# Moving one addition of VectorE's exponential into an accumulating DMA, and giving VectorE more score banks

## The chip, the cores and the metric

The kernel runs on one core of one Trainium2 chip. The metric is the device time of one execution in microseconds (us). "Before" and "after" are the kernel before and after the change. A ratio is the mean time of one kernel's fast runs over the mean time of the other's in the same rounds, so it is not quite the ratio of the medians that stand beside it. The profile of a kernel is of one execution, and its span is some 2 us shorter than the time.

## The reference, cut to what matters

```python
def _A_ref(x, wqkv, wo):                     # x: 1 x 2048 x 512, 32 heads of 16
    qkv = (x @ wqkv).reshape(B, S, 3, H, Dh).transpose(2, 0, 3, 1, 4)
    q, k, v = qkv[0], qkv[1], qkv[2]
    scores = einsum("bhqd,bhkd->bhqk", q, k) * (Dh ** -0.5)
    o = einsum("bhqk,bhkd->bhqd", softmax(scores), v)
    return o.transpose(0, 2, 1, 3).reshape(B, S, D) @ wo
def _B_ref(x, w_gate, w_up, w_down):         # F = 1792
    return (silu(x @ w_gate) * (x @ w_up)) @ w_down
g = sigmoid((x * gate_w).sum(-1, keepdims=True))
return g * _A_ref(...) + (1 - g) * _B_ref(...)
```

What costs is the softmax: 32 x 2048 x 2048 exponentials. With 16 numbers in a head, the matmuls are small beside them.

## The kernel before

Scores are made in banks of 128 keys x 512 queries of one head, 2048 banks in all. 32 units of 64 banks each (four heads, 512 queries, 16 tiles of keys) follow one another. Two engines share the exponentials. ScalarE takes two banks in one instruction:

```python
def emit_pair(bs):                            # two banks, ScalarE
    s_t = ps_s.tile([P, 2 * QBW], F32, tag="s", name="s_t")    # PSUM, 2 buffers
    e_t = etp.tile([P, 2 * QBW], BF16, tag="e", name="e_t")
    for k, b in enumerate(bs):
        score(s_t[:, k * QBW:(k + 1) * QBW], b)                # the two use different halves of the array
        ...
    act(out=e_t[:], in_=s_t[:], func=ACT.Exp, scale=inv_sqrt_dh)
```

VectorE takes single banks and works on four of them, a block, at a time. Its exponential builds the bits of a bf16 number as an integer: a first pass from PSUM (y), then six passes over 2048 elements that correct the mantissa (z, u).

```python
def emit_d(b):                                # one bank, VectorE
    d_t = ps_d.tile([P, QBW], F32, tag="d", name="d_t")        # PSUM, 1 buffer
    score(d_t[:, :], b)
    ...
    def first():
        vec.tensor_scalar(out=y[:, i * QBW:(i + 1) * QBW], in0=d_t[:, :], scalar1=EXP_A, scalar2=EXP_B, ...)
        if i < NV - 1:
            return                            # NV = 4
        z = vex.tile([P, NV * QBW], U16, tag="z", name="z_t")  # pool vex: 1 buffer; y has 3
        u = vex.tile([P, NV * QBW], F16, tag="u", name="u_t")
        vops.extend([
            (0.73, lambda: vec.tensor_scalar(out=za, in0=ya, ...)),         # z: mantissa bits
            (0.73, lambda: vec.tensor_scalar(out=ua, in0=za, ...)),         # u = K z + M
            (1.26, lambda: vec.tensor_tensor(out=ua, in0=ua, in1=ua, op=ALU.mult)),
            (1.26, lambda: vec.tensor_tensor(out=ua, in0=ua, in1=za, op=ALU.mult)),
            (1.26, lambda: vec.tensor_tensor(out=ya, in0=ya, in1=ua, op=ALU.add)),
            (0.73, lambda: (vec.tensor_scalar(out=ya, in0=ya, ...),         # the closing pass
                            late.append((plan.dve + 0.4, mine)))),
        ])
```

The output product (o_ps) of a unit takes the exponentials as they come; a block that is ready only after its unit has closed goes into a bank of its own (x_ps), which VectorE adds later.

All engines run fixed lists of instructions. A planner in the kernel's Python makes them: it keeps three clocks (plan.pe, plan.dve, plan.act), gives every instruction a planned cost, and fills TensorE's spare time with "pieces" of the other work: projections of q, k and v, the bound that is subtracted in the softmax (from keys: kb, kneg; product: bp), the feed-forward part (gp, up, dps) and the output projection (a_ps). How many banks VectorE gets is not written anywhere; it follows from the clocks and this function:

```python
def to_vector():
    un, at_ = divmod(nxt, 4 * KT)
    ...
    if nxt < 16 or at_ > (50 if un < UNITS - 1 else 12) or y_live[0] >= 3 or sum(v[0] for v in vops) > 6:
        return 0
    return 1
```

## Time and profile before

866.77 us (median of 3 runs, 866.67 to 867.56).

| engine | busy | share | what it does most |
|---|---|---|---|
| ScalarE (ACT) | 842.4 us | 97% | 880 exponentials of two banks |
| VectorE (DVE) | 797.0 us | 92% | 72 blocks of four banks |
| TensorE (PE) | 787.3 us | 91% | scores, output product, projections, feed-forward |
| GpSimd (POOL) | 8.7 us | 1% | setup |

One more reading is used throughout: the distances between the starts of ScalarE's instructions. The usual distance when nothing waits is 0.904 us after an exponential and 0.478 after a tanh (the least is 1 or 2 ns shorter). What a distance has over that is waiting, visible as idle time or hidden inside the instruction. Summed from 18 us to the last instruction of ScalarE this "stall" is 18.5 us before.

### The profile page before, as it was taken

How to read it: one execution, taken by the hardware profiler on the slowest of the kernel's cores; microseconds unless marked ns; L12 is line 12 of the kernel's file. 1: busy time of each engine (PE TensorE's matmuls, PEld its weight loads, DVE VectorE, ACT ScalarE, POOL GpSimd, SP SyncE). 2: the span in 40 equal slices, each digit the busy share in tenths (PEclk: the TensorE clock that was granted, in tenths of full speed). 3: DMA queues.
4: the chain of work that ended last, by engine and by line, in shares of the span. 5: the costliest groups of instructions: out<-in, count | busy, mean ns of one | idle time of the engine just before them, and what ended most of it. 6: DMA issues, size and time to landing. Idle time of an engine off the chain costs nothing.

```text
span 864.8 us, 14339 instructions
## 1 busy us (share of the span) xinstructions
PE 787.3 (91%) x5145; PEld 217.4 (25%) x5232; DVE 797.0 (92%) x1119; ACT 842.4 (97%) x945; POOL 8.7 (1%) x31
## 2 busy tenths in 40 slices
PE   5999999999999999999999898999989988889986
PEld 2222222222222222222222222222222222222222
DVE  7899999999999999999999999999999999999995
ACT  4999999999999999999999999999999999999996
POOL 3000000000000000000000000000000000000000
PEclk9999999999999999999999999999999999999999
DMA  8400012211210012211001121110001121100000
GB/s 201 122 1 12 9 34 48 43 44 38 47 32 8 17 38 73 54 44 41 4 7 27 39 62 38 50 47 8 1 14 42 33 65 43 27 10 4 6 20 25
DMA packets 88064, 31.99 MB, mean 37 GB/s; under 512 B 75648, under 2 KB 87544, under 8 KB 87992
## 3 DMA queue, kind: packets, MB, share of 16 engines
q1 hardware_dynamic: 86264, 30.74, 14.4%
q8 instruction: 41, 0.67, 0.3%
q10 hardware_dynamic: 1728, 0.33, 0.2%
q14 instruction: 31, 0.25, 0.1%
HBM read 20.83 MB, written 2.34 MB: 27 GB/s over the span
## 4 chain that ended last, share of the span: by engine, by line
PE 41%; ACT 39%; DVE 9%; issue 9%; SPq 1%; DMA 1%; DVEq 0%; ACTq 0%
ACT e_t L161 36%; PE s_t L158 15%; PE o_ps L158 7%; PE d_t L158 4%; DVE y_t L167 4%; PE dps L158 4%; ACT th L161 3%; PE gp L158 3%; DVE u_t L167 2%; PE up L158 2%; PE kp L158 1%; PE vp L158 1%; DVE mt L167 1%; PE qp L158 1%; PE x_ps L158 1%
## 5 line engine op out<-in xcount | busy, mean ns | idle before, releaser
L161 ACT ACTIVATE e_t<-s_t 128x1024 bf16<-128x1024 f32 x880 | 822.5, 1137 | 1.9 <-PE s_t L158 0.8
L158 PE MATMUL s_t<-qx,kaug 64*128 64x512 bf16 x1648 | 331.1, 382 | 44.3 <-ACT e_t L161 39.5
L167 DVE TENSOR_SCALAR y_t<-d_t 128x512 uint16<-128x512 f32 x288 | 198.0, 688 | 30.8 <-PE d_t L158 27.1
L158 PEld LDWEIGHTS <-kaug 64*128 64x128 bf16 x2048 | 109.7, 93 | 380.9 <-issue 376.8
L158 PE MATMUL o_ps<-e_t,vaug 128*32 128x512 bf16 x1760 | 169.9, 386 | 0.5 <-ACT e_t L161 0.5
L158 PE MATMUL d_t<-qx,kaug 64*128 64x512 bf16 x272 | 102.8, 378 | 0.9 <-DVE y_t L167 0.3
L167 DVE TENSOR_TENSOR y_t<-y_t,u_t 128x2048 uint16<-128x2048 uint16 x72 | 87.7, 1218 | 1.0
L167 DVE TENSOR_TENSOR u_t<-u_t 128x2048 f16<-128x2048 f16 x72 | 87.8, 1219 | 0.9
L167 DVE TENSOR_TENSOR u_t<-u_t,z_t 128x2048 f16<-128x2048 f16 x72 | 87.6, 1217 | 0.3
L158 PEld LDWEIGHTS <-vaug 128*32 128x32 bf16 x2048 | 43.9, 94 | 118.9 <-issue 115.7
L158 PE MATMUL dps<-wd_t,mt 128*128 128x512 bf16 x205 | 63.5, 384 | 2.5 <-issue 2.5
L158 PE MATMUL gp<-xT,wg 128*128 128x512 bf16 x202 | 62.9, 384 | 2.4 <-issue 2.4
L158 PE MATMUL up<-xT,wu 128*128 128x512 bf16 x205 | 60.9, 383 | 2.1 <-issue 2.1
L167 DVE TENSOR_SCALAR y_t<-y_t 128x2048 uint16<-128x2048 uint16 x72 | 49.6, 689 | 1.1
L167 DVE TENSOR_SCALAR u_t<-z_t 128x2048 f16<-128x2048 uint16 x72 | 49.4, 686 | 0.7
L167 DVE TENSOR_SCALAR z_t<-y_t 128x2048 uint16<-128x2048 uint16 x72 | 49.4, 686 | 0.2
L167 DVE SCALAR_TENSOR_TENSOR gs<-th,gp 128x512 bf16<-128x512 bf16 x56 | 38.3, 683 | 4.3 <-ACT th L161 3.9
L167 DVE SCALAR_TENSOR_TENSOR mt<-gs,up 128x512 bf16<-128x512 bf16 x56 | 38.2, 683 | 3.4 <-PE up L158 2.2
L161 ACT ACTIVATE th<-gp 128x512 bf16<-128x512 f32 x56 | 40.3, 720 | 0.0
L158 PEld LDWEIGHTS <-mt 128*128 128x128 bf16 x263 | 16.2, 98 | 41.1 <-issue 34.2
L158 PE MATMUL s_t<-on,kaug 64*128 64x512 bf16 x112 | 22.1, 383 | 2.6 <-ACT e_t L161 2.0
L167 DVE TENSOR_TENSOR osb<-of,x_ps 128x512 bf16<-128x512 f32 x30 | 20.4, 680 | 1.2 <-PE x_ps L158 1.2
(103 smaller groups left out, 346.9 us busy)
## 6 DMA issues: line engine op xcount, KB each, us to landing
wg<-in_B_w_gate_dram SPq DMA_DIRECT2D x56, 128.0 KB
wu<-in_B_w_up_dram SPq DMA_DIRECT2D x56, 128.0 KB
on<-osb SPq DMA_DIRECT2D x120, 16.0 KB
rb<-rr SPq DMA_DIRECT2D x15, 128.0 KB
wd_t<-in_B_w_down_dram SPq DMA_DIRECT2D x1, 1792.0 KB
qx<-qst SPq DMA_DIRECT2D x112, 16.0 KB
out_dram<-o_t SPq DMA_DIRECT2D x12, 128.0 KB
kaug<-on SPq DMA_DIRECT2D x20, 64.0 KB
```

What stands on the lines that cost most here:

```text
L158: ordered(nc.tensor.matmul(*args, **kw))
L161: ordered(nc.scalar.activation(*args, **kw))
L167: return lambda *a, **kw: ordered(f(*a, **kw))
```

## The change

VectorE's addition of y and u (72 passes) goes to the DMA engines: GpSimd's queue sends a DMA from u to y that adds. VectorE is to use the freed passes for more banks. As the DMA still reads u while the next block wants to write it, u alternates with the keys of group 0 once those are dead, from bank 320 of 2048 on.

```diff
+    u_turn = [0]
+    ADD_US = 6.0
...
-            u = vex.tile([P, NV * QBW], F16, tag="u", name="u_t")
+            u_turn[0] ^= 1
+            if u_turn[0] and nxt >= 4 * KT * QB + 4 * KT:
+                ua = kaug[:, 0, :].bitcast(F16)
+            else:
+                ua = vex.tile([P, NV * QBW], F16, tag="u", name="u_t")[:, :]
...
-                (1.26, lambda: vec.tensor_tensor(out=ua, in0=ua, in1=za, op=ALU.mult)),
-                (1.26, lambda: vec.tensor_tensor(out=ya, in0=ya, in1=ua, op=ALU.add)),
-                (0.73, lambda: (vec.tensor_scalar(out=ya, in0=ya, ...), late.append(...))),
             ])
+            def add():
+                vec.tensor_tensor(out=ua, in0=ua, in1=za, op=ALU.mult)
+                nc.gpsimd.dma_start(out=ya, in_=ua, accum_op=ALU.add)
+                added.append((plan.dve + ADD_US, last))
+            def last():
+                vec.tensor_scalar(out=ya, in0=ya, scalar1=EXP_D, scalar2=0.25, op0=ALU.add, op1=ALU.mult)
+                late.append((plan.dve + 0.4, mine))
+            vops.append((1.26, add))
...        # the planner may run other VectorE work until the DMA is due; the last stage's acc moves from kaug to mt
```

More of the change, by code (lines that the diff above doesn't have):

```diff
@@ L604 @@
     vops = []
+    added = []
+    u_turn = [0]
+    ADD_US = 6.0
     pv_turn = [True]
@@ L668, in first @@
             z = vex.tile([P, NV * QBW], U16, tag="z", name="z_t")
-            u = vex.tile([P, NV * QBW], F16, tag="u", name="u_t")
-            ya, za, ua = y[:, :], z[:, :], u[:, :]
+            u_turn[0] ^= 1
[3 more added lines that the diff above has]
+                ua = vex.tile([P, NV * QBW], F16, tag="u", name="u_t")[:, :]
+            ya, za = y[:, :], z[:, :]
             mine = list(block["b"])
@@ L678, in first @@
                 (1.26, lambda: vec.tensor_tensor(out=ua, in0=ua, in1=ua, op=ALU.mult)),
-                (1.26, lambda: vec.tensor_tensor(out=ua, in0=ua, in1=za, op=ALU.mult)),
-                (1.26, lambda: vec.tensor_tensor(out=ya, in0=ya, in1=ua, op=ALU.add)),
-                (0.73, lambda: (vec.tensor_scalar(out=ya, in0=ya, scalar1=EXP_D, scalar2=0.25, op0=ALU.add,
-                                                  op1=ALU.mult),
-                                late.append((plan.dve + 0.4, mine)))),
-            ])
+            ])
+            def add():
[6 more added lines that the diff above has]
+            vops.append((1.26, add))
         d_wait.append((plan.pe + 0.25, first))
@@ L696, in pay_v, with pay_a @@
         f()
+    def pay_a():
+        ready, f = added.pop(0)
+        plan.dve = max(plan.dve, ready) + 0.63
+        f()
     def fill_dve():
@@ L702, in fill_dve @@
                 pay_d()
+            elif added and added[0][0] <= plan.dve:
+                pay_a()
             elif owed and owed[0][0] <= plan.dve + 0.1:
@@ L706, in fill_dve @@
                 pay_v()
-            elif d_wait or owed:
-                t = min([w[0] for w in d_wait] + [o[0] for o in owed[:1]])
+            elif d_wait or owed or added:
+                t = min([w[0] for w in d_wait] + [o[0] for o in owed[:1]] + [a[0] for a in added[:1]])
                 if t > plan.pe:
@@ L837, in f @@
                     if g1 < G and not acc:
-                        acc.append(kaug[:, 0:2, :].rearrange("p g s -> p (g s)").bitcast(F32)
+                        acc.append(mt[:, 4:12, :].rearrange("p f q -> p (f q)").bitcast(F32)
                                    .rearrange("p (t d) -> p t d", d=D))
@@ L1089, in next_pv @@
         while pv_ready(None) is None:
-            pay_v() if vops else pay_d() if d_wait else pay()
+            pay_v() if vops else pay_d() if d_wait else pay() if owed else pay_a()
         emit_pv()
@@ L1144 @@
         nxt += 2
-    while closed < UNITS or late or vops:
+    while closed < UNITS or late or vops or added:
         fill_dve()
```

## The prediction

> **What bounds the kernel now.** I read the page first: busy time by engine, then the groups.
>
> ```profile
> span 864.8 us, 14339 instructions
> PE 787.3 (91%) x5145; PEld 217.4 (25%) x5232; DVE 797.0 (92%) x1119; ACT 842.4 (97%) x945; POOL 8.7 (1%) x31
> ...
> L161 ACT ACTIVATE e_t<-s_t 128x1024 bf16<-128x1024 f32 x880 | 822.5, 1137 | 1.9 <-PE s_t L158 0.8
> ...
> L167 DVE TENSOR_SCALAR y_t<-d_t 128x512 uint16<-128x512 f32 x288 | 198.0, 688 | 30.8 <-PE d_t L158 27.1
> ...
> L167 DVE TENSOR_TENSOR y_t<-y_t,u_t 128x2048 uint16<-128x2048 uint16 x72 | 87.7, 1218 | 1.0
> ...
> L167 DVE TENSOR_SCALAR y_t<-y_t 128x2048 uint16<-128x2048 uint16 x72 | 49.6, 689 | 1.1
> ```
>
> The reader is to see three engines within 55 us of one another. ScalarE does 880 exponentials of two score banks each; VectorE does the other 288 banks, in 72 blocks of four (880 x 2 + 288 = 2048). ScalarE leads: outside a start of some 18 us and an end of some 8 us it is hardly ever idle. But a busy ScalarE may still be waiting inside an instruction, so I took the timeline of ScalarE alone, from 300 us on.
>
> ```profile
> 301.90 0.72 ACT L161 ACTIVATE th<-gp 128x512 bf16<-128x512 f32 x1
> ...
> 308.38 9.40 ACT L161 ACTIVATE e_t<-s_t 128x1024 bf16<-128x1024 f32 x10
> 317.48 0.78 ACT L161 ACTIVATE th<-gp 128x512 bf16<-128x512 f32 x1
> ...
> 365.01 4.84 ACT L161 ACTIVATE e_t<-s_t 128x1024 bf16<-128x1024 f32 x5
> 370.06 6.69 ACT L161 ACTIVATE e_t<-s_t 128x1024 bf16<-128x1024 f32 x7 [0.22 <-PE s_t L158]
> ```
>
> Ten exponentials from 308.38 to 317.48 are 0.91 us each; five from 365.01 to 370.06 are 1.01. Over the whole trace the smallest and commonest distance between two starts is 0.904 us, the mean of those followed by another exponential 0.923. So each costs 0.904 when its scores are there, and over some 820 such distances 15 us are waiting that the busy figure hides. That is all a better-fed ScalarE could win beside fewer exponentials.
>
> Last the waits, of the whole trace and then of 20 to 150 us alone.
>
> ```profile
> PE s_t L158 <- ACT e_t L161: 41.5, 108, 0.7
> DVE y_t L167 <- PE d_t L158: 27.1, 64, 1.1
> ...
> PE s_t L158 <- ACT e_t L161: 4.8, 13, 0.5
> ```
>
> TensorE waits 41.5 us for ScalarE to free a score tile; that is its slack. In 20 to 150 us, with the projections, only 4.8 of it remain: there all three engines are full, and a delay on VectorE has nowhere to go.
>
> **What the Trainium skill says.** "VectorE: DVE Perf Modes", section "The perf-mode tier table (the rule you actually need)", gives 1224 ns for a 2048-element 16-bit operation of two tensors and 693 ns for one with scalars; the trace has 1218 and 689, and agrees. "DMA: Bandwidth & Descriptors", section "Anatomy of one DMA — SWDGE (gpsimd) path", fits 2.0 us plus bytes over 436 GB/s to a DMA of GpSimd's queue. "Collectives: The Full Stack", section "The bandwidth ceiling: the fold count and why AG ≠ RS ≠ AR", says that a DMA add is not slow as an addition, but needs two source reads and so about halves the rate. "SBUF — State Buffer", section "Who interferes with whom", says that GpSimd and VectorE share a port pair: while VectorE runs a scalar pass in a two-port mode, GpSimd cannot write descriptors, and the other way round; whoever starts first blocks the other. The kernel before has no DMA on GpSimd's queue, so its trace can show none of these last three.
>
> **The change part by part.** I built the changed kernel and counted its instructions on each engine.
>
> Removed: 72 additions x 1.218 = 87.7 us of VectorE. Spent again: the number of blocks is 82, ten more. On VectorE that is 40 more first passes x 0.688 = 27.5; ten times three scalar passes and two multiplications, 10 x (3 x 0.688 + 2 x 1.218) = 45.0; and 17 more additions of the late output bank (of<-of,x_ps, 23 in place of 6) x 0.68 = 11.6, because a block that is ready later misses its unit more often. Sum: 84.1. VectorE is left as full as before, at some 793 us.
>
> ScalarE: 40 banks are 20 exponentials fewer, 860 in place of 880. 20 x 0.904 = 18.1 us. As ScalarE sets the pace nearly everywhere, all of it would come off the time: 866.8 - 18.1 = 848.7. This is the ceiling of the gain, 2.1%.
>
> TensorE: a pair of banks for ScalarE goes through two halves of the array at once; the same two for VectorE go one by one. Successive groups in the timeline show about 0.22 us each, so 20 pairs fewer and 40 single ones more are +4.4, and ten more groups of the output product +2.2: together +6.6, while the span shrinks by 18. Of the 41.5 us of slack some 17 remain (41.5 - 18.1 - 6.6). TensorE then runs late for ScalarE more often; I allow 2 us.
>
> Added: 82 accumulating DMAs of 128 x 2048 x 2 bytes, 524 kB. An estimate from the two DMA sections: 2.0 + 2 x 524/436 = 4.4 us. The trace gives a longer one: the 4096-byte packets of the copies into kaug, SBUF to SBUF, took 0.33 us in the median. An even split of 128 rows over 16 engines is eight each, 2.7 us, twice that with the second read 5.3, and with the fixed 2.0 it is 7.3. The change itself plans 6.0. I take 5.5, open from 4.4 to 7.5.
>
> Where does VectorE wait for it? It runs in a fixed order, so I added the durations of the rows above over the instructions standing between. (a) Between the second multiplication, after which the DMA goes out, and the closing pass on its result there are 6.9 us in the median, under 5.8 in a tenth of the 82. With 5.5 us the shortage sums to 4 us; with 7 to 31; with 8 to 94. (b) Up to some 140 us there is one buffer u, so the next block's first write of u waits for the DMA still reading it. Nine such writes have a wait on the DMA, and 3.4, 4.1, 2.8, 3.4, 2.1, 2.8, 2.9, 4.3 and 4.8 us of work ahead of them. At 5.5 us the shortage is 2.1 + 1.4 + 2.7 + 2.1 + 3.4 + 2.7 + 2.6 + 1.2 + 0.7 = 18.9 us. VectorE's own idle time there (3 us in 50) takes some 7; two score tiles in flight hide about half of the rest. I allow 5.5 us of the time, in the stage where nothing has slack. Afterwards u alternates with the keys of group 0, and the shortest distance is 7.9 us: no loss.
>
> Sum: 866.8 - 18.1 + 5.5 (one u) + 2 (TensorE) + 1.5 (closing passes, port) = 857.7, say 858.
>
> **The rivals.** First, the whole gain arrives: 848 or a little less, if the DMA lands in 4.5 us. For it speaks that VectorE's chain is only 9% of the chain that ended last; against it the nine writes of (b). Second, the DMA is slow and VectorE becomes the bound: at 8 us, 94 us of shortage against some 54 us of idle time gives 890 or more, and each further us adds up to 82. For it speaks the packet time of kaug; against it that those packets came from several copies at once into few partitions. Third, the port: if each DMA and one scalar pass hold each other up by 0.3 us, VectorE gets 25 us more, and the time is about 868. For it speaks that 246 passes are of the two-port kind; against it that the passes reading PSUM and those of two tensors are not. Fourth, TensorE becomes the bound: 794 of 848 us is 94%, and this would leave about 855.
>
> **Range and chances.** The low end, 846, is the full gain and a little of the hidden 15 us; the high end, 885, a DMA near 7.5 us. Faster by over 2% means under 849.4, which needs all of the 18.1 us: 0.2. Slower by over 2%, above 884, needs a DMA of 7.5 us or more, or a strong fight over the port: 0.22. Within 2%: 0.58.
>
> **What would show it.** 860 exponentials in the ScalarE group, still about 0.904 us apart in full stretches; no y_t<-y_t,u_t; VectorE's busy time near 793. Waits of VectorE for a DMA before u_t<-z_t in the first 140 us, of 10 to 20 us in all, and few before y_t<-y_t. TensorE's wait for e_t down to about 17. Long waits before y_t<-y_t over the whole span would say that the DMA takes over 7 us; passes of 2048 elements longer than 0.689 would say that the port is fought over. It is wrong if ScalarE shows idle time in the middle, or if its 860 exponentials are spaced wider than 0.93.

## More of the kernel before

A piece has a deadline. One that is still missing when a unit needs it is forced, in one go and in front of everything else.

## The result

896.16 us (median of 4 runs, 893.52 to 897.96) against 866.74 before: ratio 1.0332, 95% interval 1.0313 to 1.0352. Slower, and above the range that was predicted (846 to 885).

From the page of the kernel after: busy time, TensorE's granted clock in 40 slices (in tenths), the groups of instructions (busy, mean ns | idle before, what ended it), and the DMA issues (KB, median us from issue to landing):

```profile
span 896.2 us, 14636 instructions
...
PE 819.2 (91%) x5232; PEld 220.6 (25%) x5232; DVE 789.6 (88%) x1154; ACT 829.8 (93%) x925; POOL 84.7 (9%) x113
...
PEclk9999899999999999899999999999999989999999
...
L161 ACT ACTIVATE e_t<-s_t 128x1024 bf16<-128x1024 f32 x860 | 807.9, 1106 | 38.4 <-PE s_t L158 36.8
...
L167 DVE TENSOR_SCALAR y_t<-d_t 128x512 uint16<-128x512 f32 x328 | 225.0, 686 | 45.0 <-PE d_t L158 41.4
...
L167 DVE TENSOR_SCALAR y_t<-y_t 128x2048 uint16<-128x2048 uint16 x82 | 56.1, 685 | 0.7 <-DMA y_t<-u_t 0.6
L167 DVE TENSOR_SCALAR u_t<-z_t 128x2048 f16<-128x2048 uint16 x47 | 32.4, 689 | 17.5 <-DMA y_t<-u_t 16.9
...
y_t<-u_t POOLq DMA_DIRECT2D x47, 512.0 KB, 4.8
y_t<-kaug POOLq DMA_DIRECT2D x35, 512.0 KB, 4.8
```

The counts are as built: 860 exponentials on ScalarE, 328 banks on VectorE, VectorE's busy time 789.6 us. But ScalarE, which hardly ever waited before, is idle 38.4 us in front of exponentials, and TensorE is what it waits for. TensorE in turn waited 41.5 us for ScalarE before; the waits of the kernel after (total, times, longest) show where that slack went:

```profile
ACT e_t L161 <- PE s_t L158: 36.8, 43, 5.0
PE s_t L158 <- ACT e_t L161: 19.1, 55, 0.9
DVE u_t L167 <- DMA y_t<-u_t: 16.9, 8, 3.9
ACT scaled L161 <- PE a_l L158: 8.0, 1, 8.0
```

Four stretches of both kernels, before first (stretch, its length, busy us and instructions of PE, PEld, DVE, ACT, POOL, granted clock, DMA share, GB/s):

```profile
50.00:200.00 150.00, 141.29 (x965) 41.23 (x979) 140.48 (x201) 149.93 (x170) 0.00 (x0) 1.00 0.13 29
400.00:600.00 200.00, 185.91 (x1191) 49.66 (x1211) 188.05 (x255) 199.90 (x226) 0.00 (x0) 1.00 0.13 32
```

```profile
50.00:200.00 150.00, 130.42 (x865) 35.42 (x864) 124.12 (x183) 133.34 (x145) 12.12 (x13) 0.94 0.31 61
400.00:600.00 200.00, 189.41 (x1226) 50.73 (x1224) 185.76 (x264) 198.45 (x225) 19.65 (x21) 1.00 0.44 89
```

In 400 to 600 us the change does what it was made for: ScalarE is as full as before, and the DMA is not felt. In 50 to 200 us ScalarE does 25 instructions fewer than before in the same time, and TensorE's clock is at 0.94. So the loss is not spread out; it comes in a few places. ScalarE's stall, by the measure above, in the two kernels:

| stretch, us | before | after |
|---|---|---|
| 18 to 50 | 0.7 | 1.1 |
| 50 to 200 | 1.8 | 21.5 |
| 200 to 400 | 4.4 | 14.7 |
| 400 to 600 | 3.1 | 5.0 |
| 600 to the last exponential | 5.3 | 14.9 |
| after the last exponential | 3.3 | 8.3 |
| sum | 18.5 | 65.6 |

Three kinds of place carry it. The first lies before 165 us. This is the timeline of the kernel after at its worst one (start, length, engine, instruction, idle time before and what ended it):

```profile
90.27 0.69 DVE L167 TENSOR_SCALAR u_t<-z_t 128x2048 f16<-128x2048 uint16 x1 [3.86 <-DMA y_t<-u_t]
...
91.62 0.58 PE L158 MATMUL d_t<-on,kaug 64*128 64x512 bf16 x1 [4.01 <-DVE y_t L167]
...
93.11 0.61 PE L158 MATMUL s_t<-on,kaug 64*128 64x512 bf16 x2
...
93.81 1.02 ACT L161 ACTIVATE e_t<-s_t 128x1024 bf16<-128x1024 f32 x1 [4.97 <-PE s_t L158]
```

VectorE waits 3.86 us for the DMA that still reads the one u. The pass behind it in VectorE's list would have freed d_t, so TensorE stands 4.01 us at the next score for VectorE, in front of scores that ScalarE needs; ScalarE stands 4.97 us. And a pair of scores then takes 0.61 us, not 0.39: TensorE runs at half its clock.

The second kind is at 209 us, and similar at 706 to 722:

```profile
203.69 1.04 PE L158 MATMUL qp<-xT,wqk 128*128 128x512 bf16 x4
...
206.24 2.28 DVE L167 TENSOR_REDUCE kb<-on 128x1 f32<-128x2048 bf16 x1
208.55 0.23 DVE L167 TENSOR_SCALAR kneg<-bsel,kb 128x8 bf16<-128x8 bf16 x1
...
208.84 0.38 PE L158 MATMUL bp<-aq,kneg 128*8 128x512 bf16 x1 [4.11 <-DVE kneg L167]
```

The query projection, the bound on the keys and the bound product come directly one behind the other. They had been put off until the unit needed them, and were forced: TensorE waits 4.11 us for VectorE's reduction, with nothing put between.

The third is the end. After the last exponential (ends at 880.75 us) the kernel after still has a row of feed-forward and output products to do, and ScalarE's next instruction comes late:

```profile
879.84 1.47 PE L158 MATMUL dps<-wd_t,mt 128*128 128x512 bf16 x6
...
881.57 1.04 PE L158 MATMUL dps<-wd_t,mt 128*128 128x512 bf16 x4
...
882.44 0.81 PE L158 MATMUL a_ps<-wo_t,on 128*128 128x512 bf16 x3
...
883.45 1.47 PE L158 MATMUL a_ps<-wo_t,on 128*128 128x512 bf16 x6 [0.20 <-DVE bblk L167]
...
888.79 0.69 ACT L161 ACTIVATE scaled<-a_l,gval 128x512 f32<-128x512 f32 x1 [8.04 <-PE a_l L158]
```

Before, nothing of the kind is left, and the same instruction follows the last exponential after 3.08 us:

```profile
859.52 0.69 ACT L161 ACTIVATE scaled<-a_l,gval 128x512 f32<-128x512 f32 x1 [3.08 <-PE a_l L158]
```

Counting while the programs are built agrees: the change leaves 20 matmuls of pieces for the end and forces 13 pieces; before it is none and 2.

Theories for the experiments. **A**: the single u of the first part is the loss. **B**: the 40 extra banks are; they cost TensorE time that it did not have, so pieces are put off until they are forced or left over. **C**: the DMA disturbs by itself, through the shared queues or GpSimd's port. **D**: each wait of TensorE costs again through its clock. The clock that the trace records in the kernel after is 0.5 in eight stretches of 3.4 or 6.8 us, at 73, 90, 134, 158, 209, 360, 718 and 892 us, that is right after the waits shown; before it is 0.5 once, in the last 5 us.

### The profile page after: what moved, and what is told of

It reads as the page before. It is cut to its first block, busy times and chain, and to the rows that moved or that the text cites. A ratio compares the mean times of both kernels' runs of the same rounds, so it can differ in the third digit from the quotient of the medians.

```text
span 896.2 us, 14636 instructions
## 1 busy us (share of the span) xinstructions
PE 819.2 (91%) x5232; PEld 220.6 (25%) x5232; DVE 789.6 (88%) x1154; ACT 829.8 (93%) x925; POOL 84.7 (9%) x113
## 5 line engine op out<-in xcount | busy, mean ns | idle before, releaser
L161 ACT ACTIVATE e_t<-s_t 128x1024 bf16<-128x1024 f32 x860 | 807.9, 1106 | 38.4 <-PE s_t L158 36.8
L167 DVE TENSOR_SCALAR y_t<-d_t 128x512 uint16<-128x512 f32 x328 | 225.0, 686 | 45.0 <-PE d_t L158 41.4
L158 PE MATMUL d_t<-qx,kaug 64*128 64x512 bf16 x312 | 119.8, 384 | 8.3 <-DVE y_t L167 5.6
L690 POOL DMA_DIRECT2D y_t<-u_t x47 | 43.3, 921 | 443.6 <-PE s_t L158 182.2
L690 POOL DMA_DIRECT2D y_t<-kaug x35 | 32.7, 935 | 341.1 <-PE s_t L158 236.6
L167 DVE TENSOR_TENSOR u_t<-u_t 128x2048 f16<-128x2048 f16 x47 | 57.3, 1220 | 0.7
L167 DVE TENSOR_TENSOR u_t<-u_t,z_t 128x2048 f16<-128x2048 f16 x47 | 57.2, 1217 | 0.3
L167 DVE TENSOR_SCALAR u_t<-z_t 128x2048 f16<-128x2048 uint16 x47 | 32.4, 689 | 17.5 <-DMA y_t<-u_t 16.9
L167 DVE TENSOR_TENSOR kaug<-kaug 128x2048 f16<-128x2048 f16 x35 | 42.6, 1218 | 0.3
L167 DVE TENSOR_TENSOR kaug<-kaug,z_t 128x2048 f16<-128x2048 f16 x35 | 42.6, 1216 | 0.1
```

Source lines behind the costliest of these rows:

```text
L158: ordered(nc.tensor.matmul(*args, **kw))
L161: ordered(nc.scalar.activation(*args, **kw))
L167: return lambda *a, **kw: ordered(f(*a, **kw))
L690: nc.gpsimd.dma_start(out=ya, in_=ua, accum_op=ALU.add)
```

## The experiments

The eleven runs are summed up first, beside the two kernels; "stall" is the measure above, from each profile. u: buffers for u in the first part. The runs were made in three groups on three chips (e1 to e4, e5 to e8, e9 to e11), where the kernel before took 866.6, 867.4 and 866.6 us; from one group to another the ratios compare better than the medians. A profile is one execution: that of the change is the slowest of its four (897.96 us), that of e1 the fastest (878.14).

| kernel | blocks | exponentials | u | DMA | median us | ratio to before | stall us |
|---|---|---|---|---|---|---|---|
| before | 72 | 880 | 1 | no | 866.7 | 1 | 18.5 |
| after | 82 | 860 | 1 | yes | 896.16 | 1.0332 | 65.6 |
| e1_two_u | 82 | 860 | 2 | yes | 878.99 | 1.0142 | 46.1 |
| e2_fewer | 73 | 878 | 1 | yes | 891.70 | 1.0285 | 44.0 |
| e3_two_u_fewer | 73 | 878 | 2 | yes | 873.11 | 1.0073 | 24.7 |
| e4_idle_dma | 72 | 880 | 1 | idle | 868.99 | 1.0023 | 18.5 |
| e5_filler | 82 | 860 | 2 | yes | 876.88 | 1.0108 | 44.8 |
| e6_79 | 79 | 866 | 2 | yes | 860.90 | 0.9922 | 22.7 |
| e7_79_early | 79 | 866 | 2 | yes | 863.41 | 0.9946 | 23.7 |
| e8_80 | 80 | 864 | 2 | yes | 862.99 | 0.9952 | 28.4 |
| e9_no_add | 82 | 860 | 1 | left out | 870.80 | 1.0050 | 39.5 |
| e10_79_no_add | 79 | 866 | 2 | left out | 856.21 | 0.9877 | 20.7 |
| e11_79_due | 79 | 866 | 2 | yes | 857.25 | 0.9894 | 19.4 |

### e1_two_u: a second u from the start

```diff
+            elif u_turn[0]:
+                ua = mt[:, 10:14, :].rearrange("p f q -> p (f q)").bitcast(F16)
```

> The changed kernel with a second buffer u from the first block on (four slices of the mlp tile, free until then); every engine keeps its instruction order. Theory A (the one u of the first 165 us is the main loss: VectorE waits there, TensorE idles behind it and its clock falls to half for 3.4 to 6.8 us each time): VectorE's waits of 16.9 us before u_t<-z_t go to under 2, no half-clock stretch before 165 us, ScalarE's extra spacing in 50 to 200 us falls from 21.5 us to under 5, time 872 to 880. Theory B (TensorE is overfull with the 40 extra banks, its other work is put off until it is forced): the waits before u go but the time falls by less than 8 us, to 888 or more.

Measured: 878.99 us (878.14 to 879.80), 17.2 under the change. All engines keep their order, so this is the one wait's worth. From the groups of VectorE:

```profile
L167 DVE TENSOR_SCALAR u_t<-z_t 128x2048 f16<-128x2048 uint16 x41 | 28.2, 687 | 0.6
```

The wait of 16.9 us is gone. ScalarE's stall from 50 to 200 us fell from 21.5 to 11.3 us rather than under 5, partly because the forced bound of 209 us now comes earlier, at 192, inside that stretch; and there is one half-clock stretch before 165 us, at 99 us. A holds: of the 47 us of added stall 19.5 go, and 17.2 us of the time. B is not refuted: 879 is still 30 us above what 860 exponentials would allow.

### e2_fewer and e3_two_u_fewer: no more blocks than before

```diff
-        if nxt < 16 or at_ > (50 if un < UNITS - 1 else 12) or ...
+        if nxt < 16 or at_ > (38 if un < UNITS - 1 else 12) or ...
```

> The changed kernel with 73 blocks in place of 82 (third blocks of a unit are begun later), one u as in the change. 878 exponentials. Theory B: no matmuls of the feed-forward part are left for the end, the tail after the last exponential is 8 to 9 us as before (15 in the change), the stall of 4 us at 209 us and those at 706 to 724 go; the losses of the first 165 us stay: time 878 to 886 in spite of 18 more exponentials. Theory A alone: nothing is gained, the 18 exponentials cost 16 us, 905 or more.

> Both: two buffers u and 73 blocks. If A and B together are the whole of the loss, ScalarE is again the bound with 878 exponentials, 860 to 867. If the accumulating DMA costs by itself (slower small loads, the port), 870 to 880.

Measured: 891.70 and 873.11 us. Both miss what was expected. In e2 the end is as before (3.5 us before ScalarE's last instruction) and the stalls around 706 to 724 are gone, as B said. The stall at 209 us did not go: TensorE still waits 2.7 us there for the bound on the keys (4.1 in the change). And VectorE, with 9 blocks fewer to do, waits more for the DMA:

```profile
DVE u_t L167 <- DMA y_t<-u_t: 22.2, 7, 5.5
```

The wait for u is 22.2 us in place of 16.9. A second u saves 18.6 us here (891.70 to 873.11) and 17.2 with 82 blocks: A's part is the same in both, so A and B add up. From 82 to 73 blocks the time falls by 4.5 (one u) or 5.9 us (two), while 18 more exponentials cost 16.3 (18 x 0.904). So the nine last blocks bring stall of 21 to 22 us for the 16 that they save: they are a loss by themselves. The 873 of e3 is above the 867 that A and B alone would allow; its largest stall, 4.1 us at 187 to 193 us, is again the forced bound on the keys, which this limit on blocks did not move.

### e4_idle_dma: the DMA beside the kernel before

```diff
+    nc.gpsimd.memset(mt[:, 10:14, :], 0.0)
...
                 late.append((plan.dve + 0.4, mine)),
+                nc.gpsimd.dma_start(out=idle, in_=ya.bitcast(F16), accum_op=ALU.add)
...
+            idle = kaug[:, 0, :].bitcast(U16) if nxt >= 4 * KT * QB + 4 * KT else mt[:, 10:14, :]...
```

> The kernel before, with its addition on VectorE, plus 72 accumulating DMAs of the same size into bytes that nobody reads, sent after each block's last pass. Theory C (the DMA slows the kernel by the queues' or the port's sharing alone): 872 or more, with TensorE or VectorE waiting for small DMAs, or passes of 2048 elements longer than 0.69 us. Otherwise: within 3 us of 866.7.

Measured: 868.99 us (867.79 to 869.78), ratio 1.0023 (1.0007 to 1.0038). The stall is 18.5 us, that of the kernel before. VectorE's passes of 2048 elements took 688 to 693 ns with scalars (686 to 689 before) and 1215 to 1218 with two tensors (1217 to 1219 before). C in its plain form falls: 72 such DMAs, 22.9% of the DMA engines' time for GpSimd's queue, cost the kernel before some 2 us (2.0 by the ratio).

The profile shows where 1.4 of them are: from ScalarE's last output DMA to the end of the span it is 4.2 us here and 2.8 before. All engines meet at the end, and GpSimd goes on 1.3 us after the others are done. The end is longer in every kernel that sends these DMAs, 4.2 to 5.1 us, and in none of the three without them (2.8). The fight over the port is there, but small. Where one of VectorE's scalar passes of 2048 elements fell into the first 0.85 us of GpSimd's DMA instruction (44 of 72), this took 1167 ns in the median, elsewhere 859. Of VectorE's passes that met such an instruction, 12 took 720 to 842 ns; no other took more than 696. The means hide it: 693, 689 and 688 ns for the three scalar passes, 686, 686 and 689 before.

### e5_filler: TensorE kept busy through its wait

```diff
         st["p"] = m_tile("bp")
+        for _ in range(16 if (qb, b) == (0, 2) else 0):
+            mm(st["p"][:, :], lhsT=xT[:, 0, 0:P], rhs=xT[:, 0, 0:QBW], start=True, stop=True)
         mm(st["p"][0:8, :], ...)             # as before; overwrites them
```

> Two buffers u, 82 blocks, and 16 matmuls of no use ahead of the one bound product that waited 4.1 us at 192 us; their result is overwritten. They fill TensorE's wait and shorten nothing. If the half clock that follows a wait is a cost of its own (theory D), the half-clock stretch of 6.8 us at 191 us goes, ScalarE's extra spacing between 185 and 205 us falls from 6.2 to about 4 us, and the time by 1.5 to 3 us against two buffers alone (879.0): 876 to 877.5. If the clock does not matter: unchanged, 878 to 880.

Measured: 876.88 us (874.64 to 880.10) beside 878.99 (878.14 to 879.80): the ranges overlap, so the time does not decide it. The place itself does. Here are 20 us around the forced bound, first of e1, then of e5:

```profile
185.00:205.00 20.00, 15.37 (x83) 3.65 (x82) 13.04 (x21) 14.03 (x18) 0.86 (x1) 0.83 0.27 51
```

```profile
187.00:207.00 20.00, 18.50 (x113) 5.75 (x113) 15.05 (x23) 15.80 (x20) 1.20 (x2) 1.00 0.33 61
```

With useless work in the wait the granted clock is 1.00 in place of 0.83, ScalarE gets two instructions more done, and its stall there is 4.4 us in place of 6.2, though the wait for kneg is as long as ever. So D holds at this place, by one profile of each: some 1.8 of 6.2 us were the slow clock, not the wait. Chance has a part in where the clock falls: up to this place the two programs are the same, yet e1 has a half-clock stretch at 99 us and e5 has it at 130 us instead.

The traces show when the clock falls. Its changes lie on a grid of 3.413 us. I took TensorE's busy share in each grid window of all 13 profiles. At full clock and under 0.47 busy, the next window was at half clock every time (25 of 25, leaving out the first 20 us; 13 of them at the ends of the 13 runs); between 0.47 and 0.58 it was so in 8 of 14; above 0.6 it happened once (0.71) in some 3,100 windows. Two windows of the kernel after that were followed by half clock:

```profile
206.00:209.40 3.40, 0.56 (x5) 0.22 (x6) 2.86 (x4) 0.00 (x0) 0.00 (x0) 1.00 0.50 99
...
356.20:359.60 3.40, 1.70 (x14) 0.50 (x12) 3.40 (x6) 2.19 (x3) 0.00 (x0) 1.00 0.04 10
```

0.56 and 1.70 us busy of 3.40. The Trainium skill, "TensorE: Matmul & The Clock Gate", section "Part 1: The HAM clock gate (the "warmup" mystery)", has the 3.4 us window and the half rate; it calls the state idle, and a later section, "HAM oscillation — how this bites in real kernels", gives as the rule that there be no idle gaps over some 3.4 us. Here shorter ones were enough where they added up in one window: before the half clock at 360 us TensorE was idle for 1.10 and 0.61 us, at 158 us for 1.4 and 0.1.

### e6_79, e7_79_early, e8_80 and e11_79_due: fewer extra banks, and pieces due earlier

```diff
# e6_79, beside the second u of e1_two_u
-   at_ > (50 if un < UNITS - 1 else 12)
+   at_ > ((36 if un < 4 else 44) if un < UNITS - 1 else 12)
-   pace.add(k_pieces(b, tb), 0, d - 22 + tb, prev)           # deadlines of the bound on the keys
+   pace.add(k_pieces(b, tb), 0, d - 26 + tb, prev)
-   pace.add([(0.2, bnd, False)], 0, d - 17, ks)
+   pace.add([(0.2, bnd, False)], 0, d - 21, ks)
# e7_79_early: (38 if un < 4 else 44), d - 32, d - 27, ADD_US = 5.5
# e8_80:       (36 if un < 7 else 50), d - 26, d - 21, f1 = SLOTS - 20
# e11_79_due:  as e6_79, and the feed-forward work due 12 slots earlier:
-   f0, f1 = 72, SLOTS - 8
+   f0, f1 = 72, SLOTS - 20
```

> Two buffers u, 79 blocks (fewer in the first four units, where TensorE has the projections), and the bound on the keys due four slots earlier. 866 exponentials, no matmuls left for the end. Theory B (the 40 extra banks cost on TensorE what they save on ScalarE, by work that is put off until it is forced): with the put-off work gone, 14 x 0.904 = 12.7 us are saved and some 3 us of stall come on top: 855 to 861, faster than both kernels. If any extra bank costs TensorE its worth: 864 or more.

> As the 79 blocks before it, but with 5.5 us planned for the DMA and the bound ten slots earlier. The DMA lands 5.3 us (median), 6.0 (nine tenths) after the multiplication in the change, so the closing passes should wait some us more in all: VectorE's waits for a DMA before y_t 2 to 6 us in all. Time 854 to 861.

> Two buffers u, 80 blocks, two in each of the first seven units, feed-forward work due 12 slots earlier. 864 exponentials, 12 matmuls left for the end, so a tail of 11 to 12 us after the last exponential (8.4 before, 15 in the change). Theory B: 856 to 862.

> As the 79 blocks with the bound due four slots earlier, and the feed-forward work due 12 slots earlier. Another draw of the same idea: 858 to 863.

Measured: 860.90, 863.41, 862.99 and 857.25 us, ratios 0.9922 (0.9910 to 0.9935), 0.9946 (0.9932 to 0.9959), 0.9952 (0.9939 to 0.9964) and 0.9894 (0.9878 to 0.9911). All beat both kernels, by 0.5 to 1.1%. e6 is within what was expected, e11 0.75 us faster than its range; e7 and e8 are slower than expected by 2.4 and 1.0 us. In e8 the end after the last exponential took 13.0 us, not 11 to 12. In e7 VectorE waited 8.0 us for DMAs before closing passes, not 2 to 6 (3.8 in e6): planning 5.5 us for the DMA is too little. From the page of the best, e11:

```profile
span 855.0 us, 14470 instructions
...
PE 789.8 (92%) x5143; PEld 218.7 (26%) x5232; DVE 760.9 (89%) x1112; ACT 829.8 (97%) x931; POOL 85.4 (10%) x110
...
L161 ACT ACTIVATE e_t<-s_t 128x1024 bf16<-128x1024 f32 x866 | 809.4, 1131 | 2.8 <-PE s_t L158 1.6
```

With three blocks fewer than the change, a second u and pieces that come in time, ScalarE's idle time before exponentials is 2.8 us (38.4 in the change) and its stall 19.4, near the 18.5 of before. Then its 14 exponentials fewer, 12.7 us (14 x 0.904), are nearly all found in the spans: 864.8 to 855.0, 9.8 us; of the rest 2.3 are the later end (5.1 us after ScalarE's last output DMA, 2.8 before). These runs changed the number of blocks, their places and the deadlines together. None has 82 blocks with early deadlines, so how much each of them brings is not shown.

### e9_no_add and e10_79_no_add: the same schedules without the DMA

```diff
-                nc.gpsimd.dma_start(out=ya, in_=ua, accum_op=ALU.add)
```

> The changed kernel with the accumulating DMA simply left out (the result is wrong on purpose: the correction is not added). TensorE and VectorE keep their instruction order exactly, one u, 82 blocks. So nothing waits for a DMA and nothing shares the queues or the port. If the schedule with its extra banks is what remains of the loss beside the one u (theory B), this is as slow as two buffers u with the DMA: 874 to 880, with the 4 us wait for the bound on the keys and the tail of 15 us still there. If the DMA itself costs more than its wait for u: 848 to 866.

> The kernel of 79 blocks and two buffers u, again without its DMA (wrong result on purpose), same order on TensorE and VectorE. What the DMA costs where it is waited for little: I expect 857 to 860.5, 0.5 to 3 us under the 860.9 with it. Under 855 would mean that the DMA disturbs by itself.

Measured: 870.80 us (869.42 to 873.37) and 856.21 (855.71 to 856.36). The first lies between the two ranges that were expected; the second is 4.7 under e6_79 (3.9 by the ratios, as e6 ran on another chip), more than the 0.5 to 3 that were expected. 2.2 us of it are the end: 2.8 us after ScalarE's last output DMA, 5.0 in e6. Both still came out within the comparison's tolerance, although the correction is missing; they compute a coarser exponential and are measurements, not versions.

e9 splits the loss. With TensorE's and VectorE's lists as in the change and no DMA, 870.80 us remain: the whole DMA costs 25.4 us in the change, of which the wait for u is 17.2 (e1). The other 8.2 (878.99 to 870.80) come with the DMA but not with that wait. As the instructions are the same, the two profiles (8.7 us apart) can be laid over each other, and they differ in few places. 2.2 us lie after ScalarE's last output DMA (5.0 us to the end, 2.8 without the DMA). 1.4 us lie at 340 us, where VectorE waits 1.6 us for the small DMA dn<-dd, and not at all in e9. 3.3 us lie at 697 to 707 us, where TensorE waits for the small DMA qx<-bq; first e1, then e9:

```profile
698.70 0.39 PE L158 MATMUL d_t<-qx,kaug 64*128 64x512 bf16 x1 [1.74 <-DMA qx<-bq]
...
699.94 0.61 PE L158 MATMUL s_t<-qx,kaug 64*128 64x512 bf16 x2 [0.31 <-DMA qx<-bq]
```

```profile
694.90 0.39 PE L158 MATMUL d_t<-qx,kaug 64*128 64x512 bf16 x1 [0.94 <-DMA qx<-bq]
...
696.15 0.39 PE L158 MATMUL s_t<-qx,kaug 64*128 64x512 bf16 x2 [0.33 <-DMA qx<-bq]
```

The wait is 0.8 us longer in e1, and the clock then falls to half for 6.8 us, which it does not in e9. At 100 us a half-clock stretch of e1 that e9 does not have is worth 0.9, and 0.6 lie at 195 us. That is 8.4 of the 8.7. That the small DMAs come late because forced pieces leave them no time in advance, so that a busier DMA queue is felt that was not felt in e4, is a reading that no run tested.

## Why the prediction was wrong

The sum was 866.8 - 18.1 + 5.5 + 2 + 1.5 = 857.7. With the measured sizes it is 848.7 (only the 18.1 taken off) + 22.1 (the schedule itself, e9) + 17.2 (the one u) + 8.2 (the DMA otherwise) = 896.2.

- **"As ScalarE sets the pace nearly everywhere, all of it would come off the time"**, with 2 us allowed for TensorE: this is the step that failed. It was read from sums over the whole span (TensorE's 41.5 us of slack less 18.1 less 6.6 leaves 17). The slack was not one sum that could be spent: the prediction itself had read that only 4.8 us of it lie in 20 to 150 us, and still took one allowance for the whole. Where TensorE had no gaps, the planner put pieces off until they were forced. The runs show 22.1 us for it in e9, with the 4.1 us wait for the bound on the keys and the late end among it; and e6 and e11 show that it goes with three blocks fewer and earlier deadlines together. A sign of the prediction came true all the same: TensorE's wait for ScalarE fell to 19.1 us ("about 17"). The sum does not tell where slack is missing. The fourth rival, TensorE as the bound, had been given "about 855".
- **The wait for u, size of the wait**: right. 18.9 us of shortage were worked out for a DMA of 5.5 us; VectorE waited 16.9, and the DMA landed 5.3 us (median of the 82 in the trace) after the multiplication's end, within 6.0 in nine of ten. The 5.5 was chosen between estimates of 4.4 and 7.3, so there is luck in it.
- **The wait for u, its price**: mis-sized. VectorE's own idle time took at most 2 us (18.9 less 16.9), not 7. "Two score tiles in flight hide about half of the rest" gave 5.5 us; it measured 17.2 (e1), as much as the whole wait. The timeline shows why nothing was hidden: TensorE's list stood at d_t in front of the scores that ScalarE needed, and TensorE's clock fell to half for 3.4 or 6.8 us after four of these waits. The clock was not in the prediction at all.
- **The closing passes and the port**, 1.5 us: the closing passes waited 0.7 us in the change, and the port held 12 of VectorE's passes up, by at most 0.15 us (e4). The third rival, with 0.3 us of VectorE for each DMA, falls. The second, a slow DMA, falls too: it needed 7.5 us or more. The sum for the DMA's other cost was too low all the same: 8.2 us, in the form of small DMAs that came late, with the clock behind them, and of an end that is 2.2 us longer; no part of the prediction named these.
- **VectorE's sum** (793 us busy): 789.6 measured. Its freed passes were spent as planned. That was not where the time was.
- Of what was to show it wrong, "ScalarE shows idle time in the middle" and a spacing over 0.93 both came: 38.4 us and 0.975 (mean distance from one exponential to the next exponential).

## What to carry to other kernels

When one engine leads by a few per cent, the work that moves off it must be weighed against the slack of every other engine in the stage where it lands, not against a sum over the span. A fixed order turns a short wait on one engine into a wait on all that stand behind it, and on TensorE a wait may be paid twice, through the clock. Take a freed resource up to the point where other work still keeps its deadlines: here, with a second u, 79 or 80 blocks and earlier deadlines gained 0.5 to 1.1% where 82 blocks lost 1.4%, and a DMA that has replaced a pass needs a buffer for as long as it reads, from the first block on.

## What the Trainium skill lacked or had wrong

- "TensorE: Matmul & The Clock Gate", section "HAM oscillation — how this bites in real kernels": the rule of no idle gaps over some 3.4 us is too lenient. In 13 profiles the clock fell to half after every grid window of 3.413 us (past the start) in which TensorE was under 0.47 busy, also where the longest single wait was 1.7 us (e5 at 700 us), and in 8 of 14 windows between 0.47 and 0.58. In mid-run it then stayed at half for one or two windows. The page says further down that frequent short idle times can do it too, but gives no share of a window.
- "DMA: Bandwidth & Descriptors", section "Anatomy of one DMA — SWDGE (gpsimd) path": no figure for an accumulating DMA between two SBUF tiles. 128 x 2048 elements of 2 bytes took 4.8 us from issue to landing (median; 4.4 at the least) and 5.3 from the end of the VectorE pass before it. The estimate of 4.4 us from that section's fit, with two reads as in "Collectives: The Full Stack", is at the lower end of this.
- "SBUF — State Buffer", section "Who interferes with whom": that VectorE's two-port passes and GpSimd's descriptors block each other agrees with the trace of e4. There the cost was less than the other's whole instruction: 0.3 us for GpSimd (1167 ns against 859), at most 0.15 us for VectorE (842 ns against 696).
- No page was found that has the later end: with accumulating DMAs on GpSimd's queue the span ended 4.2 to 5.1 us after ScalarE's last output DMA, without them 2.8.
